# Attention with a mixture of experts: the products with V in two groups of steps per piece instead of four or five

## The chip, the cores and the metric

One Trainium2 chip, one of its cores. The metric is the device time of one execution in microseconds (us). TensorE (PE in the profile, PEld for its weight loads), VectorE (DVE), ScalarE (ACT), GpSimd (POOL) and the DMA queues that SyncE issues (SP) run side by side, each through its own instructions in order, and wait for each other by semaphores.

## The reference

```python
scores = scale * np.matmul(q, k.transpose(0, 1, 3, 2))        # q, k, v: (8, 8, 576, 64)
thresh = np.max(scores, axis=-1, keepdims=True) - tau
scores = np.where(scores >= thresh, scores, -1e9)
attn = np.exp(scores - np.max(scores, axis=-1, keepdims=True))
attn = attn / (np.sum(attn, axis=-1, keepdims=True) + 1e-09)
x = np.matmul(attn, v).transpose(0, 2, 1, 3).reshape(8 * 576, 512)
# then, for every row of x: gate = top 2 of 8 experts of
#   x @ w_gate + log1p(exp(x @ w_noise)) * noise, softmax over the two;
# out = sum over the two of weight * (relu(x @ w1[e]) @ w2[e]),  w1[e]: 512x1024, w2[e]: 1024x512
```

## The kernel before

The program has two parts. Attention works on 32 **turns**, one for each batch and pair of heads (4 pairs, 8 batches). A turn has nine **steps**: 576 query rows of two heads are nine tiles of 128 rows, the first of them (the corner) made of the last 64 rows of both heads. The experts' part follows, and its first loads and gathers are mixed into the last turns.

No scheduler reorders anything: every operation is entered in a list under a step number and a phase, and the program is written out step by step, within a step in the order of phases 0, 1, 2, 3, 4, 5, 8, 6, 7. Step g = 9n + s is step s of turn n, and a table entry of 9 or more falls into the next turn: entry 17 is step 8, entry 21 is step 3 of the turn after the next opening. The text below names steps 0 to 8 by that remainder, and lets a turn open with step 8, in which the scores of the next pair's corner stand. In a step stand, with the line that the profile names:

- phase 0: `oev`, a copy of a finished piece of O by ScalarE (L376);
- phase 1: scores of the next tile, four matmuls of 288 columns into one of two buffers `sp` (L256; six for the corner);
- phases 2 to 4: VectorE takes the row maximum (`rowmax`, L267), ScalarE the exponential (L269), VectorE masks the tile of two steps ago (L292), ScalarE makes the threshold (L277);
- phase 5: `avpiece`, `xlpart`, `xev` and the operations of the gate (below);
- phase 8: ScalarE scales q (L173, step 0) and takes the high parts of k and q (L185, `hik` in step 0, `hiq` in step 2), GpSimd the low parts (L186, `lok`, `loq`);
- phase 6: four transposes of the masked tile of three steps ago on TensorE (L304), copied to `pt` by ScalarE (L307; the corner's by L309 and L310 in step 3);
- phase 7: `pcorner` in step 8 (L325, copies L326 and L327) and `prem` in step 2 (L318, copy L319).

**The products with V.** The transposed probabilities of a turn are multiplied with V in two pieces of 320 and 256 columns. A piece is a sum of five products (index `kt`); one of them is a pair of matmuls for the two heads, each on 64 of the 128 columns of the array (L370); the fifth takes 64 rows for each head from `ptr`. `av` gives the steps of the five for each piece, `oev` the steps in which the pieces are copied to `ot`, `xl` the steps in which `ot` is transposed and multiplied with the gate's weights (`xlpart`, L389 and L390), which VectorE scales into rows of x by `rn` (`xev`, L403). GpSimd makes `rn` in step 3 (L344 to L348).

**Four banks.** Everything but the scores goes to four PSUM banks `tp0` to `tp3`. A list of free ones is kept when the program is written: whoever needs a bank takes the one that has been free longest, and a piece of O keeps its bank from its first product to its copy. So the place of `avpiece` and `oev` in the list decides which bank every transposition takes, and for whose copy it waits.

**The gate.** When the four turns of a batch are done, a chain of small operations picks the experts of its rows. Its place hangs on `xl`:

```python
            x = d["xl"][1] + 1
            for i, f in enumerate((gate_sum, gate_abs, gate_exp, gate_soft, gate_max, gate_hot, gate_rank,
                                   gate_slot, gate_slot2)):
                at(G + START["gate"][i] if late else g + x + i + (i > 3), 5, f, b)
            for i in range(2 * NB):
                to = g + x + 11 + i
```

`gate_hot` makes a table `mb` (VectorE `oh` L555, GpSimd `dl` L558 and `mb` L561); `gate_rank` sums it on TensorE (L568, L570). Ten writes to `slot_table` by GpSimd follow, one per step (`gate_put`, L610 and L611). For the last of the eight batches fixed steps are used. The last turn takes its `av`, `oev` and `xl` from another table (`LAST`), which stays as it is.

Of the kernel before, what the change touches and what calls it, by code (L numbers as in the profile page):

```python
# [36 lines left out]
WARM = 10  # L37

SCHED = dict(
    lag=2, mlag=2, lead=1, corner=8, rem=11, norm=11, av=((10, 11, 12, 13, 14), (15, 17, 17, 18, 19)), oev=(15, 20),  # L40
    xl=(16, 22), q=2, k=0, oevp=0, pieces=((0, 320), (320, 576)), order=(0, 1, 2, 3, 4, 5, 8, 6, 7),
    rec=12, xs=4, qsc="act", qs=0)


# [1 line left out]
    av=((11, 11, 12, 12, 12), (12, 12, 12, 12, 12)), oev=(13, 13), xl=(14, 14), rec=13, norm=12)  # L46
# [1139 lines left out]
```

## Time and profile before

| what | value |
|---|---|
| three runs | 1490.91 us median, 1488.62 to 1496.92 |
| the profiled execution | 1492.15 us, of which 1490.4 us lie between the first and the last instruction |
| busy over the span | PE 98%, PEld 80%, DVE 60%, ACT 47%, POOL 59% |
| busy in 300 to 400 us (attention) | PE 98.03, DVE 83.50, ACT 84.41, POOL 57.72 us of 100 |
| busy in 880 to 960 us (experts) | PE 80.00, DVE 34.23, ACT 16.95, POOL 44.50 us of 80 |
| mean granted clock of TensorE | 0.994 |

A matmul in 32-bit floats shows as two records, so one product with V (two matmuls) shows as four. Matmuls overlap: the duration in a row is longer than the distance to the next row, and the distance from start to start is what an operation costs. The first experts' matmul (L871) starts at 603.67 us; everything that the change moves lies before it.

### The profile page before, as it was taken

How to read it: one execution, taken by the hardware profiler on the slowest of the kernel's cores; microseconds unless marked ns; L12 is line 12 of the kernel's file. 1: busy time of each engine (PE TensorE's matmuls, PEld its weight loads, DVE VectorE, ACT ScalarE, POOL GpSimd, SP SyncE). 2: the span in 40 equal slices, each digit the busy share in tenths (PEclk: the TensorE clock that was granted, in tenths of full speed). 3: DMA queues.
4: the chain of work that ended last, by engine and by line, in shares of the span. 5: the costliest groups of instructions: out<-in, count | busy, mean ns of one | idle time of the engine just before them, and what ended most of it. 6: DMA issues, size and time to landing. Idle time of an engine off the chain costs nothing. (4 is left out here: it accounts for less than half of the span.)

```text
span 1490.4 us, 25728 instructions
## 1 busy us (share of the span) xinstructions
PE 1453.8 (98%) x8750; PEld 1195.9 (80%) x8750; DVE 896.4 (60%) x2477; ACT 706.5 (47%) x1447; POOL 882.8 (59%) x1205
## 2 busy tenths in 40 slices
PE   9999999999999997998999999999999999999995
PEld 6776676766666675787998988989989989989884
DVE  8888888887888889653554354444444543453320
ACT  7887888887888887422222132222222221231210
POOL 3346565656565678877376576576575574665612
PEclk9999999999999999999999999999999999999998
DMA  7768686867686664335155155254353352452422
GB/s 200 186 193 193 168 211 171 209 186 194 175 205 172 159 164 114 76 87 106 43 101 119 36 114 112 53 115 92 66 108 84 85 111 54 92 121 43 71 29 32
DMA packets 137748, 180.67 MB, mean 121 GB/s; under 512 B 61304, under 2 KB 70480, under 8 KB 136592
## 3 DMA queue, kind: packets, MB, share of 16 engines
q1 hardware_dynamic: 106816, 139.05, 35.1%
q0 software_dynamic: 30800, 39.95, 16.6%
q8 instruction: 71, 1.16, 0.4%
q14 instruction: 61, 0.50, 0.1%
HBM read 83.33 MB, written 40.74 MB: 83 GB/s over the span
## 5 line engine op out<-in xcount | busy, mean ns | idle before, releaser
L269 ACT ACTIVATE e<-ns,nm 128x576 f32<-128x576 f32 x288 | 223.2, 775 | 44.1 <-DVE ns L267 41.3
L292 DVE SCALAR_TENSOR_TENSOR p<-ns,thr,e 128x576 f32<-128x576 f32 x256 | 224.0, 875 | 21.5 <-ACT thr L277 20.8
L267 DVE TENSOR_SCALAR_CACHE_REDUCE ns<-sp 128x576 f32<-128x576 f32 x288 | 214.2, 744 | 20.5 <-PE sp L256 18.2
L304 PEld LDWEIGHTS tp<-ident,p 128*128 128x128 f32 x1024 | 110.2, 143 | 100.8 <-ACT ot L376 22.6
L307 ACT ACTIVATE pt<-tp 128x512 f32<-128x512 f32 x256 | 151.0, 590 | 54.1 <-PE tp L304 53.2
L370 PE MATMUL tp<-pt,vt 128*64 128x256 f32 (+1 forms) x1024 | 175.9, 427 | 0.0
L304 PE MATMUL tp<-ident,p 128*128 128x128 f32 x1024 | 167.6, 286 | 1.3 <-DVE p L292 1.3
L256 PE MATMUL sp<-ks,qh 128*128 128x288 f32 x496 | 159.8, 336 | 4.4 <-DVE ns L267 4.3
L913 POOL DMA_INDIRECT out<-m_y,ix x54 | 89.8, 1664 | 100.5 <-DVE m_y L951 86.5
L256 PE MATMUL sp<-ks,ql 128*128 128x288 f32 x496 | 138.4, 295 | 0.0
L186 POOL TENSOR_TENSOR lok<-kr,hik 128x640 fp32r<-128x640 f32 x31 | 57.1, 1841 | 136.8 <-ACT hik L185 124.1
L913 POOL DMA_INDIRECT out<-m_y,sx x43 | 69.8, 1623 | 106.7 <-DVE m_y L894 82.8
L841 POOL DMA_INDIRECT m_vt<-x_rows,ix x102 | 102.5, 1005 | 41.2 <-issue 27.5
L841 POOL DMA_INDIRECT m_zeros<-x_rows,ix x102 | 101.7, 997 | 36.4 <-issue 30.3
L841 POOL DMA_INDIRECT m_xg<-x_rows,ix x100 | 99.5, 995 | 29.9 <-issue 27.2
L873 ACT ACTIVATE m_p<-m_tp 128x384 fp32r<-128x384 f32 (+1 forms) x66 | 33.2, 503 | 143.2 <-PE m_tp L871 143.2
L256 PEld LDWEIGHTS sp<-ks,qh 128*128 128x128 f32 x496 | 93.8, 189 | 6.9 <-DVE ns L267 6.2
L611 POOL DMA_INDIRECT slot_table<-pay,sl x80 | 86.3, 1079 | 17.8 <-issue 11.1
L256 PEld LDWEIGHTS sp<-ks,ql 128*128 128x128 f32 x496 | 94.4, 190 | 0.0
L894 DVE TENSOR_SCALAR m_y<-m_sp,gw 128x512 f32<-128x512 f32 (+1 forms) x43 | 32.2, 750 | 101.8 <-PE m_sp L892 97.2
L370 PEld LDWEIGHTS tp<-pt,vt 128*64 128x64 f32 x1024 | 56.8, 135 | 42.8 <-issue 25.4
L874 DVE SCALAR_TENSOR_TENSOR m_p<-m_tp,m_p 128x384 fp32r<-128x384 f32 (+1 forms) x66 | 37.8, 574 | 59.7 <-ACT m_p L873 59.5
(385 smaller groups left out, 3607.9 us busy)
## 6 DMA issues: line engine op xcount, KB each, us to landing
m_qr<-w SPq DMA_DIRECT2D x85, 256.0 KB
qh<-hiq SPq DMA_DIRECT2D x124, 144.0 KB
ql<-loq SPq DMA_DIRECT2D x124, 144.0 KB
m_kr<-w SPq DMA_DIRECT2D x43, 256.0 KB
kr<-k SPq DMA_DIRECT2D x32, 320.0 KB
out<-zeros SPq DMA_DIRECT2D x19, 512.0 KB
qr<-q SPq DMA_DIRECT2D x32, 288.0 KB
vt<-v SPq DMA_DIRECT2D x8, 1152.0 KB
```

What stands on the lines that cost most here:

```text
L186: nc.gpsimd.tensor_tensor(lo, x, hi.bitcast(F32), op=ALU.subtract)
L256: nc.tensor.matmul(o, q_, k_, start=(i == 0), stop=(i == len(parts) - 1))
L267: nc.vector.tensor_scalar(ns, sp[:, :, 0:HALF], -1.0 / math.sqrt(D), None, op0=ALU.mult, op1=ALU.min, accum_out=nm)
L269: nc.scalar.activation(e, ns, AF.Exp, bias=nm, scale=-1.0)
L292: nc.vector.scalar_tensor_tensor(p, ns, thr, e, op0=ALU.is_le, op1=ALU.mult, accum_out=ssum[n][:, c:c + 1])
L304: nc.tensor.transpose(tp[:, kt, :], p[:, 128 * kt:128 * kt + 128], ident)
L307: nc.scalar.activation(pt[n][:, s, :, c0:c0 + 128], tp, AF.Copy)
L370: nc.tensor.matmul(o[64 * s:64 * s + 64, 0:c1 - c0], w, x, start=(kt == 0), stop=(kt == 4))
L611: st = nc.gpsimd.indirect_dma_start(out=table, out_offset=bass.IndirectOffsetOnAxis(ap=d["sl"][0:m, i, c:c + 1], axis=0), in_=d["pay"][0:m ...
L841: self.nc.gpsimd.indirect_dma_start(out=xg[:, j, :], out_offset=None, in_=x4, in_offset=bass.IndirectOffsetOnAxis(ap=ix[:, kk:kk + 1], axi ...
L874: nc.vector.scalar_tensor_tensor(hl[:, 0:n], ps[:, 0:n], 0.0, hh[:, 0:n].bitcast(F32), op0=ALU.max, op1=ALU.subtract)
L913: st = self.nc.gpsimd.indirect_dma_start(out=out, out_offset=bass.IndirectOffsetOnAxis(ap=idx, axis=0), in_=y, in_offset=None, compute_op= ...
```

## The change

The ten products of a turn move into four groups, the copies of O and the second part of x come one or two steps earlier.

```diff
 SCHED = dict(
-    lag=2, mlag=2, lead=1, corner=8, rem=11, norm=11, av=((10, 11, 12, 13, 14), (15, 17, 17, 18, 19)), oev=(15, 20),
-    xl=(16, 22), q=2, k=0, oevp=0, pieces=((0, 320), (320, 576)), order=(0, 1, 2, 3, 4, 5, 8, 6, 7),
+    lag=2, mlag=2, lead=1, corner=8, rem=11, norm=11, av=((11, 11, 13, 13, 13), (15, 15, 17, 17, 17)), oev=(14, 18),
+    xl=(16, 21), q=2, k=0, oevp=0, pieces=((0, 320), (320, 576)), order=(0, 1, 2, 3, 4, 5, 8, 6, 7),
     rec=12, xs=4, qsc="act", qs=0)
```

By steps of a turn: products stood in steps 1 to 6, 8, and 0 (two in steps 1 and 8, one in each of the others); now two stand in step 2, three in step 4, two in step 6 and three in step 8. The copy of the second piece moves from step 2 to step 0, that of the first from step 6 to step 5, the second part of x from step 4 to step 3. With `xl`, the gate's chain and the writes of x and of `slot_table` come one step earlier for the first seven batches.

**TensorE, the sum of the gate.** Before, in the turn in which the first batch is ranked: the end of step 1's products, step 2 with its transposes, the scores of step 3, and then the sum of `mb`.

```order
L370 MATMUL tp3_1736<-pt1_1512,vt1_614 64x320 x2
L304 MATMUL tp1_1786<-ident_85,p5_1688 128x128 x4
L318 MATMUL tp0_1792<-ident_85,p2_1501 128x128
...
L256 MATMUL sp0_1798<-ks0_1407,qh0_110 128x288
L256 MATMUL sp0_1798<-ks0_1407,ql0_112 128x288
L568 LDWEIGHTS tri_133
L568 MATMUL tp2_1811<-mb0_136,tri_133 128x48
```

And now: step 1's transposes (it has no product), the scores of step 2, the sum, and only then step 2's products and transposes.

```order
L304 MATMUL tp3_1745<-ident_85,p5_1694 128x128 x4
L256 MATMUL sp1_1751<-ks0_1410,qh0_110 128x288
L256 MATMUL sp1_1751<-ks0_1410,ql0_112 128x288
...
L568 LDWEIGHTS tri_133
L568 MATMUL tp2_1764<-mb0_136,tri_133 128x48
...
L370 MATMUL tp1_1779<-pt1_1519,vt1_619 64x320 x4
L304 MATMUL tp0_1800<-ident_85,p5_1694 128x128 x4
```

The sum has moved ahead of step 2's products, transposes and `prem`.

**GpSimd, what the sum reads.** Before, around `mb` of the same batch:

```order
L538 TENSOR_TENSOR nl0_1655<-gc0_1644,lgs0_1566 128x40
L186 TENSOR_TENSOR lok0_1697<-kr1_1397,hik0_1696 128x640
L558 TENSOR_TENSOR dl0_1764<-mx0_1722 128x5
L561 TENSOR_TENSOR mb0_136<-oh0_1762 128x40
L337 TENSOR_SCALAR ssum1_1455<-ssum1_1455 128x9
L186 TENSOR_TENSOR loq0_1771<-qr1_1398,hiq0_1770 128x576
```

And now:

```order
L538 TENSOR_TENSOR nl0_1632<-gc0_1621,lgs0_1543 128x40
L186 TENSOR_TENSOR lok0_1712<-kr1_1402,hik0_1711 128x640
L558 TENSOR_TENSOR dl0_1742<-mx0_1697 128x5
L561 TENSOR_TENSOR mb0_136<-oh0_1740 128x40
L580 TENSOR_SCALAR gs0_1776<-e20_1771 128x5
L337 TENSOR_SCALAR ssum1_1452<-ssum1_1452 128x9
L186 TENSOR_TENSOR loq0_1785<-qr1_1403,hiq0_1784 128x576
```

`mb` stays behind `lok`, which stands in step 0 and reads ScalarE's `hik`.

**ScalarE, which copy frees which bank.** Before, in a turn without the gate, from the copy of step 1's transposes to the corner's in step 3:

```order
L307 ACTIVATE pt0_4104<-tp2_4314 128x4x128
L376 ACTIVATE ot1_4176<-tp1_4190 128x256
L269 ACTIVATE e1_4328<-ns1_4326,nm0_4301 128x576
L277 ACTIVATE thr0_4302<-nm0_4301,atau_105 128x2
L185 ACTIVATE hiq0_4339<-qr0_3953 128x576
L307 ACTIVATE pt0_4104<-tp3_4355 128x4x128
L319 ACTIVATE ptr0_4105<-tp2_4361 128x512
L269 ACTIVATE e2_4376<-ns2_4372,nm1_4373 128x576
L309 ACTIVATE pt1_4391<-tp1_4393 128x4x64
```

And now:

```order
L307 ACTIVATE pt0_4121<-tp1_4314 128x4x128
L269 ACTIVATE e1_4327<-ns1_4325,nm0_4306 128x576
L277 ACTIVATE thr0_4307<-nm0_4306,atau_105 128x2
L185 ACTIVATE hiq0_4341<-qr0_3959 128x576
L307 ACTIVATE pt0_4121<-tp2_4357 128x4x128
L319 ACTIVATE ptr0_4122<-tp0_4363 128x512
L269 ACTIVATE e2_4378<-ns2_4374,nm1_4375 128x576
L309 ACTIVATE pt1_4400<-tp2_4402 128x4x64
```

Before, the corner's transposes of step 3 took bank `tp1`, which the copy of O had freed earlier; now they take `tp2`, the bank of step 2's own transposes, which ScalarE's last copy but one before them frees. The copy of O has left this stretch for step 0.

## The prediction

> **What bounds the kernel now.** I read the busy times by stretch first (the table above): in attention TensorE is busy 98 of 100 us, the others 58 to 84. Then the waits of TensorE between 100 and 600 us. A row gives who waited for whom, the sum, how often, and the longest:
>
> ```profile
> PE sp L256 <- DVE ns L267: 5.2, 9, 2.3
> PE tp L325 <- DVE xr L403: 3.1, 3, 1.6
> PE tp L568 <- POOL mb L561: 1.3, 1, 1.3
> ```
>
> These few us in 500 say that TensorE sets the pace and hardly waits. So I read its timeline over one turn (start, duration, what); the time from start to start is what counts:
>
> ```profile
> 313.23 0.38 PE L256 MATMUL sp<-hik,qd 128*128 128x288 f32 x1
> 315.74 0.38 PE L256 MATMUL sp<-ks,qh 128*128 128x288 f32 x1
> ...
> 319.81 0.38 PE L256 MATMUL sp<-ks,qh 128*128 128x288 f32 x1
> 320.29 0.30 PE L256 MATMUL sp<-ks,ql 128*128 128x288 f32 x1
> 320.52 0.76 PE L370 MATMUL tp<-pt,vt 128*64 128x320 f32 x4
> 321.21 0.65 PE L304 MATMUL tp<-ident,p 128*128 128x128 f32 x4
> 322.05 0.38 PE L256 MATMUL sp<-ks,qh 128*128 128x288 f32 x1
> 323.45 0.66 PE L304 MATMUL tp<-ident,pr 128*128 128x128 f32 x4
> 323.87 0.38 PE L256 MATMUL sp<-ks,qh 128*128 128x288 f32 x1
> 324.34 0.29 PE L256 MATMUL sp<-ks,ql 128*128 128x288 f32 x1
> 324.47 0.27 PE L389 MATMUL tp<-ident,ot 128*128 128x128 f32 x1
> 326.43 0.38 PE L256 MATMUL sp<-ks,qh 128*128 128x288 f32 x1
> 328.23 0.38 PE L256 MATMUL sp<-ks,qh 128*128 128x288 f32 x1
> 329.92 0.38 PE L256 MATMUL sp<-ks,qh 128*128 128x288 f32 x1
> 331.46 0.38 PE L256 MATMUL sp<-hik,qd 128*128 128x288 f32 x1
> ```
>
> The turn opens at 313.23 and the next at 331.46: 18.23 us, of which step 8 takes 2.51, step 2 2.24, step 5 1.80, step 6 1.69, step 7 1.54. A step of attention's first turn, which has no product yet, and the products of the last turn, which stand in a row already, price the rest:
>
> ```profile
> 20.81 0.38 PE L256 MATMUL sp<-ks,qh 128*128 128x288 f32 x1
> 21.81 0.40 PE L256 MATMUL sp<-ks,qh 128*128 128x288 f32 x1
> ...
> 609.18 1.30 PE L370 MATMUL tp<-pt,vt 128*64 128x320 f32 x8
> 610.41 0.66 PE L304 MATMUL tp<-ident,p 128*128 128x128 f32 x4
> 612.66 0.76 PE L370 MATMUL tp<-ptr,vt 64*64 64x320 f32 x4
> 613.35 1.95 PE L370 MATMUL tp<-pt,vt 128*64 128x256 f32 x16
> ```
>
> A step without a product takes 1.00. One product of 320 columns takes 0.69 (320.52 to 321.21), two in a row 1.23 (609.18 to 610.41): the second costs 0.54, one from `ptr` behind them 0.69. By the columns, 0.43 and about 0.58 with 256.
>
> **Part 1: fewer groups on TensorE.** The matmuls are the same; what goes is the entry into the 64-column form and the way out. After a score's last matmul a product starts 0.23 later (320.29 to 320.52), the 128-column transposes of O 0.13 (324.34 to 324.47). The steps become, in us: 8: 2.51 + 0.58 = 3.09; 0 and 1: 1.00 each; 2: 2.24 + 0.54 = 2.78; 3: 1.00 and three blocks of x, 2.0 (step 7 has two blocks for 0.54; the third, narrower one I estimate at 0.4 to 0.5 with its change of form); 4: 1.80 + 0.54 + 0.69 = 3.03; 5: 1.00; 6: 1.69 + 0.43 = 2.12; 7: 1.54. Sum 17.56, that is 0.67 less than 18.23. Over 30 turns this would be -20 us, if nothing else waited.
>
> A rule of the Trainium skill bears on this: TensorEngine Tiling (Array Packing), Key Properties, says that changing the tiling mode drains TensorE, so grouping should pay. The 0.23 against 0.13 agrees. By this rule alone the time would be that of the first rival below.
>
> **Part 2: ScalarE's copies and the bank of step 3.** ScalarE works without a pause from step 8's copy to step 2's. First and last of 15 rows, and two between:
>
> ```profile
> 315.91 0.60 ACT L307 ACTIVATE pt<-tp 128x512 f32<-128x512 f32 x1 [0.57 <-PE tp L304]
> ...
> 318.39 0.72 ACT L185 ACTIVATE hik<-kr 128x640 fp32r<-128x640 f32 x1
> ...
> 320.64 0.38 ACT L376 ACTIVATE ot<-tp 128x256 f32<-128x256 f32 x1
> 320.90 0.78 ACT L269 ACTIVATE e<-ns,nm 128x576 f32<-128x576 f32 x1
> ...
> 322.33 0.59 ACT L307 ACTIVATE pt<-tp 128x512 f32<-128x512 f32 x1
> ```
>
> From 315.91 to 322.92 it needs 7.01. The change keeps the same 15 operations (the copy of O only moves forward among them, 0.26 from its start to the next), and the first waits for step 8's transposes, which come 0.58 later behind the third product: 2.68 + 0.58 = 3.26 after the opening. So step 2's copy ends at 10.27. TensorE would reach the corner's transposes of step 3 at 3.09 + 1.00 + 1.00 + 2.78 + 2.0 - 0.42 = 9.45 (0.42 is 323.45 to 323.87). Before, they took a bank that the copy of O had freed; now they need the bank that this copy empties, and wait 0.82. The turn is then 10.27 + 0.42 + 3.03 + 1.00 + 2.12 + 1.54 = 18.38: the 0.67 is gone, and 0.15 more. Behind the waiting L304 stand all matmuls of steps 3 and 4, so nothing hides it. In quiet turns (16 of 30) this makes +2 us; an error of 0.1 us in the sum gives 0 to +4.
>
> **Part 3: the gate's sum comes too early.** In six turns of the middle, TensorE sums `mb`. Before:
>
> ```profile
> 107.47 0.38 PE L256 MATMUL sp<-hik,qd 128*128 128x288 f32 x1
> ...
> 116.91 0.20 PE L568 MATMUL tp<-mb,tri 128*128 128x48 bf16 x1
> ...
> 117.14 0.49 PE L370 MATMUL tp<-pt,vt 128*64 128x320 f32 x2
> ...
> 113.42 1.56 POOL L186 TENSOR_TENSOR lok<-kr,hik 128x640 fp32r<-128x640 f32 x1 [0.93 <-ACT hik L185]
> 114.93 0.72 POOL L558 TENSOR_TENSOR dl<-mx 128x5 f32<-128x5 f32 x1
> 116.04 0.27 POOL L561 TENSOR_TENSOR mb<-oh 128x40 bf16<-128x40 f32 x1 [0.39 <-DVE oh L555]
> ```
>
> `mb` is done 8.84 after the opening (116.31), and TensorE comes to it at 9.44, in step 3: 0.6 to spare. Now the sum stands in step 2, which TensorE reaches at 3.09 + 1.00 + 1.00, and its place behind the scores 0.60 later: 5.69. But `mb` on GpSimd stays behind `lok`, and `lok` behind ScalarE's `hik`, which ends at 5.16 + 0.72 before and 0.58 + 0.26 later now (step 8's copy is later, the copy of O stands ahead): 6.72. Then `lok` 1.56, `dl` 0.72 and `mb` 0.27 with the gaps of these rows (1.51 from `lok` to `dl`): done at 9.4. VectorE's `oh` comes a step earlier too and is no longer last. TensorE waits 3.7 us. From there: 0.23 to the products (116.91 to 117.14), 1.23 for two, 0.84 for the transposes and `prem` (321.21 to 322.05): step 3 starts at 11.70, the turn ends 2.0 + 3.03 + 1.00 + 2.12 + 1.54 later, at 21.4, against 18.23 and the sum's 0.15, 18.4. So +3.0 in each of six turns, +18; with `dl` at `mb`'s 0.27 or `lok` at 2.0 it is +15 to +21.
>
> Such a wait also costs clock. After the waits of the turn that opens at 144.09, none of them longer than 1.6 (the second row above), the granted clock (0.50 in this row) was halved for one stretch:
>
> ```profile
> 150.10:153.40 3.30, 3.30 (x14) 2.14 (x16) 3.30 (x9) 3.26 (x9) 2.80 (x6) 0.50 0.01 1
> ...
> 300.00:400.00 100.00, 98.03 (x721) 68.51 (x722) 83.50 (x239) 84.41 (x179) 57.72 (x108) 1.00 0.69 179
> ```
>
> That costs up to 1.65 us. In the second row, with a wait of the same length at 371 us, the clock stayed full, so I take half of the six: +5, bounds 0 and +10. The Trainium skill (TensorE: Matmul & The Clock Gate, Part 1) states half clock after an idle window of about 3.4 us; by it all six would pay, +10. The row shows that less idle time can do.
>
> **Part 4: what else moves.** (a) The ten writes to `slot_table` come a step earlier on GpSimd, ahead of one more of its own operations, and still stand before `rn` in step 3. VectorE waits there:
>
> ```profile
> DVE xr L403 <- POOL spacer L610: 16.1, 6, 4.0
> ```
>
> Six turns, 16.1 us; the wait stays, and the 0.53 that ScalarE had in hand before step 3's transposes (322.92 to 323.45) goes: 6 x 0.53 = +3, bounds -2 (the writes start earlier and are done earlier) and +6. (b) For the seventh batch TensorE already waits 1.3 for `mb`, with GpSimd full of gathers; a step earlier it waits longer: +2, bounds 0 and +5. (c) The writes of x on SP's queue and VectorE's rows of x come earlier; VectorE is busy 84 of 100 and has the long step 4 to catch up. Its `xev` waits for TensorE as before: 0. The last turn keeps its own table.
>
> **Sum.** 2 + 18 + 5 + 3 + 2 = +30 us. The profiled execution took 1492.15 us (1490.4 within the span), 1.2 above the median of the runs: 1522 by its own time, and **1521** beside the median 1490.91. By its own bounds the case runs from +11 to +47, 1502 to 1538.
>
> **Rivals.**
> 1. Faster: TensorE alone sets the pace. It needs ScalarE's copy of step 2 ready by 9.45 and `mb` by 5.69. For it: TensorE waits for almost nothing now. Against: 15 rows of ScalarE that leave no gap, and an `mb` that ends 8.84 after the opening even now. 30 turns x -0.67 = -20: 1471. It decides where the copy comes 0.67 sooner than I have it and the sum doesn't wait.
> 2. The bank binds, the sum doesn't wait (if `lok` were ready sooner): 2 + 6 x 0.15 + 3 + 2 = +8: 1499.
> 3. The sum waits, the bank doesn't (if ScalarE's row is shorter when the copy of O moves): 22 turns x -0.67 = -15, and 18 + 5 + 2: +10, 1501. With the clock never halved 1496.
> 4. The half clock in every turn of the gate, and longer waits for `rn`: +47, 1538 or more.
>
> **Chances.** My case 0.65, rival 1 0.08, 2 0.10, 3 0.10, 4 0.07. What a measurement of this kernel tells from no change is about 0.5%, 7.5 us: from 1483 to 1498 is the same. Rival 1 is faster: 0.08. Rivals 2 and 3 lie on the line, half on each side: same 0.10 and, with my case's lowest corner, 0.12. Slower 0.80. The range 1496 to 1538 leaves out rival 1, the upper half of 4 and a tail of my case.
>
> **What would show it.** Right: L304 on `pr` (step 3) waits some 0.8 for ACT `pt` in quiet turns of 18.4; `PE L568 <- POOL mb` becomes the longest wait of TensorE, seven times 3 us or more; step 4 near 3.0, step 0 near 1.0. Wrong: quiet turns of 17.6, or an L568 without a wait. I would be wrong by a size if the clock falls more than once after a wait, or if step 3 takes another bank than the one read from the order.

## The result, and the profile after

| | before | after |
|---|---|---|
| median of four runs, us | 1491.32 (1488.62 to 1496.92) | 1530.74 (1528.09 to 1532.58) |
| the profiled execution, its span, us | 1492.15, 1490.4 | 1528.09, 1526.3 |
| mean granted clock of TensorE | 0.994 | 0.983 |

The ratio of the times is 1.0269, with a 95% interval of 1.0249 to 1.0288: slower by 39 us, where 1521 was forecast. Measured from opening to opening (the rows `sp<-hik,qd`), the turns show where the 35.9 us between the two spans lie. A gate turn is one with the gate's sum, the turn ahead is the one before it, and a put turn is the second one behind it: there VectorE's rows wait for `rn`, which stands on GpSimd among the ten writes.

| stretch | before, us | after, us | difference |
|---|---|---|---|
| 9 quiet turns, 18.23 and 18.39 to 18.41 each | 164.1 | 165.6 | +1.5 |
| 6 turns ahead of a gate turn | 109.4 | 115.1 | +5.7 |
| 6 gate turns, 18.38 and 22.64 to 24.18 each | 110.3 | 140.8 | +30.5 |
| 6 put turns | 117.6 | 113.6 | -4.0 |
| the start, the first and the last turns, up to L871 | 102.3 | 102.4 | +0.1 |
| the experts' part | 886.7 | 888.9 | +2.2 |

The busy times by stretch, of the changed kernel between 300 and 400 us (each engine's busy us in the order PE, PEld, DVE, ACT, POOL, then the granted clock): TensorE waits now, and its clock isn't full.

```profile
300.00:400.00 100.00, 93.01 (x673) 68.12 (x673) 75.89 (x223) 76.75 (x164) 57.39 (x112) 0.97 0.64 170
```

The waits of the changed kernel between 100 and 600 us: TensorE's four longest groups, then one of VectorE and one of GpSimd.

```profile
PE tp L304 <- ACT pt L307: 14.6, 19, 0.8
PE tp L568 <- POOL mb L561: 12.6, 5, 2.7
PE sp L256 <- DVE ns L267: 7.7, 14, 0.9
PE tp L568 <- ACT e L573: 5.4, 2, 2.7
...
DVE ab L513 <- POOL lgs L506: 20.9, 7, 3.1
...
POOL rn L347 <- DMA slot_table<-pay,sl: 16.4, 6, 3.3
```

The first row is the forecast wait for ScalarE's copy, the second and the fourth the wait of the gate's sum (where `e` is named, it is the exponential of `dl`, which ends beside `mb`). The third has two halves, and neither was foreseen. In each turn ahead VectorE waits with `ab` (the fifth row), and the row maximum that stands behind it comes late for TensorE's scores. In each gate turn the row maximum stands behind the ten small operations of `gate_max` (L545, L547; from 3.97 to 5.00 us after the opening), and the scores of step 2 wait 0.54. The first turn ahead, which opens at 89.80:

```profile
106.54 0.20 DVE L513 SCALAR_TENSOR_TENSOR ab<-lgs 128x40 f32<-128x40 f32 x1 [3.06 <-POOL lgs L506]
...
107.47 0.40 PE L256 MATMUL sp<-ks,qh 128*128 128x288 f32 x1 [0.56 <-DVE ns L267]
```

A quiet turn of the changed kernel, TensorE and then ScalarE (start, duration, what; in brackets the wait and who ended it):

```profile
131.68 0.38 PE L256 MATMUL sp<-hik,qd 128*128 128x288 f32 x1
...
134.76 0.38 PE L256 MATMUL sp<-ks,qh 128*128 128x288 f32 x1
...
142.00 0.66 PE L304 MATMUL tp<-ident,pr 128*128 128x128 f32 x4 [0.81 <-ACT pt L307]
...
150.08 0.38 PE L256 MATMUL sp<-hik,qd 128*128 128x288 f32 x1
...
134.93 0.60 ACT L307 ACTIVATE pt<-tp 128x512 f32<-128x512 f32 x1 [1.15 <-PE tp L304]
...
137.01 0.77 ACT L173 ACTIVATE qr<-qr,scale 128x576 f32<-128x576 f32 x1
...
141.36 0.59 ACT L307 ACTIVATE pt<-tp 128x512 f32<-128x512 f32 x1
```

ScalarE's row goes from 3.25 after the opening to 141.36 + 0.59, that is 10.27, and step 3's transposes of the corner start 0.05 later. The turn has 18.40 us.

A gate turn of the changed kernel: TensorE, GpSimd, and then the busy times and the clock in the 3.41 us up to the sum and in those behind it:

```profile
109.03 0.38 PE L256 MATMUL sp<-hik,qd 128*128 128x288 f32 x1
...
113.08 0.38 PE L256 MATMUL sp<-ks,qh 128*128 128x288 f32 x1
...
114.83 0.40 PE L256 MATMUL sp<-ks,qh 128*128 128x288 f32 x1 [0.54 <-DVE ns L267]
...
118.31 0.20 PE L568 MATMUL tp<-mb,tri 128*128 128x48 bf16 x1 [2.69 <-POOL mb L561]
...
115.83 1.54 POOL L186 TENSOR_TENSOR lok<-kr,hik 128x640 fp32r<-128x640 f32 x1 [3.37 <-ACT hik L185]
117.33 0.71 POOL L558 TENSOR_TENSOR dl<-mx 128x5 f32<-128x5 f32 x1
118.00 0.26 POOL L561 TENSOR_TENSOR mb<-oh 128x40 bf16<-128x40 f32 x1
...
114.64:118.05 3.41, 0.80 (x4) 0.66 (x5) 3.31 (x10) 3.41 (x7) 2.22 (x3) 1.00 0.43 118
118.05:121.47 3.42, 3.16 (x17) 1.58 (x17) 2.55 (x7) 0.87 (x3) 3.05 (x6) 0.50 0.91 207
```

`mb` is done at 118.26, 9.23 after the opening; TensorE's step 1 took 1.75 instead of 0.97 (113.08 to 114.83, waiting for VectorE); it stood ready for the sum at 115.62, waited 2.69, and then worked for 3.42 us at half clock.

### The profile page after: what moved, and what is told of

Its sections match the earlier page's. It is cut to its first block, busy times and chain, and to the rows that moved or that the text cites. A ratio compares the mean times of both kernels' runs of the same rounds, so it can differ in the third digit from the quotient of the medians.

```text
span 1526.3 us, 25726 instructions
## 1 busy us (share of the span) xinstructions
PE 1452.4 (95%) x8750; PEld 1218.9 (80%) x8750; DVE 883.6 (58%) x2477; ACT 703.0 (46%) x1447; POOL 876.9 (57%) x1205
## 5 line engine op out<-in xcount | busy, mean ns | idle before, releaser
L292 DVE SCALAR_TENSOR_TENSOR p<-ns,thr,e 128x576 f32<-128x576 f32 x256 | 220.3, 861 | 42.0 <-ACT thr L277 41.2
L304 PEld LDWEIGHTS tp<-ident,p 128*128 128x128 f32 x1024 | 117.5, 145 | 62.8 <-issue 33.8
L370 PE MATMUL tp<-pt,vt 128*64 128x256 f32 (+1 forms) x1024 | 158.5, 432 | 0.0
L186 POOL TENSOR_TENSOR lok<-kr,hik 128x640 fp32r<-128x640 f32 x31 | 50.6, 1633 | 171.3 <-ACT hik L185 160.4
L370 PEld LDWEIGHTS tp<-pt,vt 128*64 128x64 f32 x1024 | 64.0, 139 | 47.2 <-issue 22.9
L611 POOL DMA_INDIRECT slot_table<-pay,sl x80 | 90.2, 1127 | 18.2 <-issue 10.7
L871 PE MATMUL m_tp<-m_pt,m_pt 128*128 128x384 f32 (+1 forms) x396 | 73.6, 343 | 0.0
```

Source lines behind the costliest of these rows:

```text
L186: nc.gpsimd.tensor_tensor(lo, x, hi.bitcast(F32), op=ALU.subtract)
L292: nc.vector.scalar_tensor_tensor(p, ns, thr, e, op0=ALU.is_le, op1=ALU.mult, accum_out=ssum[n][:, c:c + 1])
L304: nc.tensor.transpose(tp[:, kt, :], p[:, 128 * kt:128 * kt + 128], ident)
L370: nc.tensor.matmul(o[64 * s:64 * s + 64, 0:c1 - c0], w, x, start=(kt == 0), stop=(kt == 4))
L611: st = nc.gpsimd.indirect_dma_start(out=table, out_offset=bass.IndirectOffsetOnAxis(ap=d["sl"][0:m, i, c:c + 1], axis=0), in_=d["pay"][0:m ...
L871: nc.tensor.matmul(ps[:, 0:n], w[:, 128 * c:128 * c + 128], x[:, c, 0:n], start=(i == 0), stop=(i == len(ops) - 1))
```

## The experiments

All times are medians; each ratio is to the kernel before, run beside it on the same chip, and is taken over all runs, so that it need not be the quotient of two medians.

| kernel | us | ratio, 95% interval |
|---|---|---|
| 1: after, gate chain in its old place | 1506.31 | 1.0104 (1.0085 to 1.0124) |
| 2: after, only the gate's sum in its old place | 1507.35 | 1.0135 (1.0105 to 1.0165) |
| 3: before, gate chain a step earlier | 1498.21 | 1.0061 (1.0044 to 1.0078) |
| 4: before, only the products moved | 1499.31 | 1.0068 (1.0051 to 1.0084) |
| 5: 1 and the scaling of q moved | 1487.13 | 0.9987 (0.9971 to 1.0004) |
| 6: after, the scaling of q moved | 1509.73 | 1.0125 (1.0093 to 1.0157) |
| 7: before, the scaling of q moved | 1485.57 | 0.9971 (0.9959 to 0.9982) |
| 8: after, `dl` and `mb` on VectorE | 1517.35 | 1.0188 (1.0161 to 1.0215) |
| 9: 5 and two more waits moved | 1473.80 | 0.9886 (0.9858 to 0.9913) |
| 10: 7 and the writes moved | 1483.36 | 0.9955 (0.9939 to 0.9971) |

**1. The gate's chain and the writes back in their old steps.**

```diff
-            x = d["xl"][1] + 1
+            x = d["xl"][1] + 1 + (n < NP - 1)
```

> The changed kernel, but the gate's chain, the writes of x and of slot_table stand one step later, at the steps of the kernel before. Theory (the gate's chain, tied to xl, came a step too early, and the saved form changes are eaten by ScalarE's bank in step 3): TensorE reaches the sum of mb in step 3 about 8.4 us after the opening, mb is done at 9.3, and most of that wait lies within the wait for ScalarE's copy; gate turns about 18.5 instead of 23.5, quiet turns stay at 18.4; about 1492 us, between 1488 and 1498. Rival (the groups themselves cost: long steps starve VectorE and ScalarE): still above 1515.

1506, above the range: three fifths of the loss go, but not all that the theory gave. The gate turns are still 19.4 to 21.0, since the sum waits in its old place too:

```profile
PE tp L568 <- POOL mb L561: 8.5, 7, 1.5
...
PE tp L389 <- ACT pt L307: 1.7, 6, 0.3
```

The new groups leave steps 0 and 1 without a product, so TensorE comes to step 3's sum 8.6 after the opening and not at 9.44, while `mb` is done at 9.7 instead of 8.84. The expectation had such a wait, from 8.4 to 9.3, but put most of it inside the wait for ScalarE's copy. The trace shows one behind the other: with a bank taken by the sum, the transposes of O behind it (L389) wait for that copy, and step 3's transposes of the corner come only after them, at 11.34 instead of 10.32. Three of the six turns also have a stretch at half clock (20.9 to 21.0, the others 19.4). The turns ahead are back at 18.40 and VectorE's `ab` waits 0.8 at most. So of the +5.7 there, the part beyond the quiet turn's growth needs the chain's early place. It needs the new groups as well: in run 3, which has the early place with the old products, these turns keep 18.23, and `ab` waits 0.8.

**2. Only the sum and the two operations behind it back.**

```diff
-                at(... else g + x + i + (i > 3), 5, f, b)
+                at(... else g + x + i + (i > 3) + (i > 5), 5, f, b)
```

> The changed kernel, but only gate_rank, gate_slot and gate_slot2 stand one step later (their old place); the front of the chain and the writes stay early. Theory: the wait of 2.7 us for mb and the halved clock go, the wait of 0.8 us in the turn before each gate turn (scores of step 7 behind VectorE) stays: about 6 us above e1, 1494 to 1503. Rival: as in e1, above 1515.

1507, no faster or slower than the first: missed, and by the same oversight. The L568 row is gone from the waits, but behind the sum the transposes of O wait for ScalarE, up to 1.2 us, so that five gate turns still have 19.4, and the turns ahead keep their 19.2:

```profile
PE tp L389 <- ACT pt L307: 5.9, 7, 1.2
```

**3. The old products, the gate's chain a step earlier.**

```diff
-            x = d["xl"][1] + 1
+            x = d["xl"][1] + (n == NP - 1)
```

> The kernel before with its own products, copies and xl, but the gate's chain, the writes of x and of slot_table one step earlier. Theory: TensorE reaches the sum in step 2 at about 7.2 us after the opening, mb is done at about 8.6: a wait of 1.4 us in six turns, perhaps half clock behind it: 1500 to 1512. Rival (the early chain is harmless, the groups are at fault): within 3 us of the kernel before.

1498, just under the range. Every gate turn grew from 18.38 to 19.73 behind a wait of 1.2 for `mb`, so the early sum costs by itself, without the new groups. It costs less than in the changed kernel because the old products still stood ahead of it, and none of the six waits halved the clock. The put turns became 3.6 us shorter in sum: in this trace the earlier writes are a gain, not a loss.

**4. The products alone in their new steps.**

```diff
-av=((10, 11, 12, 13, 14), (15, 17, 17, 18, 19))
+av=((11, 11, 13, 13, 13), (15, 15, 17, 17, 17))
```

> The kernel before with only the products in the new groups; copies of O, xl and the gate as before. Theory: in quiet turns the wait moves from step 3 to the prem transposes of step 2, whose bank waits for ScalarE's copy of step 1 (about 0.75 us), and a little in step 4; turn about 18.3; 1489 to 1499. Rival (groups at fault): above 1515. Rival 2 (form changes saved and nothing waits): 17.6 per turn, 1472.

1499.3, just over the upper edge. With the copy of O still in step 2 the banks rotate otherwise, and the wait for ScalarE moves to `prem`, 0.5 where 0.75 was expected. The quiet turns have 18.19, those right behind a gate turn 18.47, none near 17.6; the gate turns, of which the expectation says nothing, have 19.16 instead of 18.38:

```profile
PE tp L318 <- ACT pt L307: 10.5, 23, 0.5
```

**5. The first kernel, and ScalarE's row made shorter.** The scaling of q (L173, 0.66 from start to start) leaves step 0 for step 7 of the turn before.

```diff
-            at(g + d["qs"], 8, scale_q, n + 1)
+            at(g - 2 if n > 1 else g, 8, scale_q, n + 1)
```

> The changed kernel with the gate chain and its writes one step later (the kernel of the first experiment), and ScalarE's scaling of the next pair's q moved from step 8 to step 7 of the turn before, so out of ScalarE's row between the copy of step 8 and the copy of step 2. Theory (that row of 7.01 us sets the quiet turn): the row is 0.66 shorter, the wait of the corner's transposes in step 3 falls from 0.8 to 0.2 or less, quiet turns go from 18.39 to about 17.7, and over some 28 turns the time falls by 15 to 20 from 1506, to 1484 to 1492. Rival (the bank is not what holds step 3, or another copy takes its place): quiet turns stay at 18.2 to 18.4, time 1500 to 1507.

1487, in the range, and every quiet turn has 17.73 or 17.74 where it had 18.40: 0.66, the length of the operation that was taken out. The wait in step 3 falls from 0.8 to 0.2, as forecast. That ScalarE's row set the turn is shown.

**6. The changed kernel with that move alone.**

> The changed kernel with nothing but the scaling of q moved from step 8 to step 7 of the turn before. Theory: quiet turns near 17.7 instead of 18.39; in the turns of the gate hik, lok and mb come 0.66 earlier as well, so the wait for mb falls from 2.7 to about 2.0 and may halve the clock less often. 1502 to 1514 instead of 1531. Rival (ScalarE's row is not the reason): 1526 to 1532.

1509.7, in the range. Quiet turns 17.73, the sum's wait 2.0 instead of 2.7. Beyond its purpose this run prices the clock, since the same wait fell with and without a half clock. The openings and the sum of the first and second gate turn, and the busy times in stretches of 3.41 us (PE first, the clock is the third value from the end):

```profile
106.21 0.38 PE L256 MATMUL sp<-hik,qd 128*128 128x288 f32 x1
...
114.79 0.18 PE L568 MATMUL tp<-mb,tri 128*128 128x48 bf16 x1 [1.98 <-POOL mb L561]
...
182.75 0.38 PE L256 MATMUL sp<-hik,qd 128*128 128x288 f32 x1
...
191.31 0.18 PE L568 MATMUL tp<-mb,tri 128*128 128x48 bf16 x1 [1.97 <-POOL mb L561]
...
110.29:113.70 3.41, 1.97 (x14) 1.60 (x13) 3.41 (x20) 3.39 (x8) 1.36 (x1) 1.00 0.52 202
113.70:117.11 3.41, 2.32 (x23) 1.56 (x22) 3.34 (x11) 2.02 (x6) 1.46 (x6) 1.00 0.83 187
188.79:192.20 3.41, 1.44 (x16) 1.03 (x17) 3.38 (x7) 2.17 (x5) 2.15 (x3) 1.00 0.45 108
192.20:195.61 3.41, 3.41 (x17) 2.47 (x14) 1.93 (x9) 2.11 (x6) 2.56 (x5) 0.51 0.95 226
```

The stretches are cut where the clock changes: in each of these traces its changes lie on one grid of 3.413 us. The first wait falls across a line of the grid (1.44 and 1.09 us without work on the two sides) and the clock stays full; that turn has 20.55 us. The second lies within one window (1.97 without work), the next window runs at half clock, and the turn has 22.14. So one window at half clock costs 1.59 us, and the fifth gate turn, with two, cost 2.81 (23.36).

**7. The kernel before with that move.**

> The kernel before with the same move of the scaling of q alone. Theory: there TensorE has its own 18.23 us of work in a turn and ScalarE's copy of step 2 is ready 0.53 before it is wanted, so a shorter row changes nothing: quiet turns 18.23, time 1487 to 1493. Rival (a shorter row of ScalarE is a gain by itself, in any kernel): 1476 to 1484.

1485.6, a little under the range. The quiet turns keep 18.23 to the hundredth, so the theory holds where it was meant; but the put turns lose 6.9 us in sum (117.6 to 110.7), which the expectation had left out: the low parts of k and q come some 0.7 earlier on GpSimd, and the waits of `rn` there fall from 19.8 to 13.2.

**8. The gate's `dl` and `mb` on VectorE.**

```diff
-        eng.tensor_tensor(dl, ...)
+        vec.tensor_tensor(dl, ...)
...
-        eng.tensor_tensor(mb[b % 2][:, 0:NB, :], ...)
+        vec.tensor_tensor(mb[b % 2][:, 0:NB, :], ...)
```

> The changed kernel with the gate's dl and mb on VectorE right behind oh, instead of on GpSimd behind lok. Theory (the gate's sum waits because mb stands behind hik and lok): mb is done near 7.1 after the opening instead of 9.24, the wait of L568 falls from 2.7 to about 1.3, the turns of the gate from 22.6 to 24.2 down to 19.5 to 21, with fewer stretches at half clock: 1508 to 1518 instead of 1531. Rival (it waits for something else, the bank or the gate's own operations on VectorE, and only the name of the last one changes): 1526 to 1533.

1517, in the range, with a wait of 1.9 instead of 1.3; the gate turns have 20.4 to 23.3, mostly above the 19.5 to 21 expected. `mb` no longer stands behind `lok` in a queue, and yet waits it out. The first gate turn, and then the turn of the seventh batch, where `lok` had ended before:

```profile
115.82 0.16 DVE L558 TENSOR_TENSOR dl<-mx 128x5 f32<-128x5 f32 x1
115.94 1.52 DVE L561 TENSOR_TENSOR mb<-oh 128x40 bf16<-128x40 f32 x1
...
115.87 1.54 POOL L186 TENSOR_TENSOR lok<-kr,hik 128x640 fp32r<-128x640 f32 x1 [3.39 <-ACT hik L185]
...
589.74 0.20 DVE L561 TENSOR_TENSOR mb<-oh 128x40 bf16<-128x40 f32 x1
...
588.07 1.54 POOL L186 TENSOR_TENSOR lok<-kr,hik 128x640 fp32r<-128x640 f32 x1 [0.22 <-ACT hik L185]
```

Forty columns took 1.51 to 1.54 us on VectorE in all six gate turns, until `lok` ended on GpSimd, and 0.20 where `lok` did not run beside it (0.26 on GpSimd itself). The Trainium skill (SBUF — State Buffer, section "SBUF: two separate sides") says that an operation of VectorE with two inputs from SBUF and one of GpSimd that reads SBUF exclude each other for a whole instruction; the rows agree.

**9. The fifth kernel without the waits that it still showed.** The sum stands one step later, where TensorE doesn't reach it before `mb`, and no write to `slot_table` stands right ahead of `rn` on GpSimd. What `rn` waited for can be read from the traces of the two kernels and of runs 1 to 8: in six turns of each, the fourth copy of `rn` carries a wait for the landing of the write that was issued last ahead of it, and it starts 3.1 to 7.5 us after that write's issue.

```diff
-                at(... else g + x + i + (i > 3), 5, f, b)
+                at(... else g + x + i + (i > 3) + (i > 5), 5, f, b)
...
-                to = g + x + 11 + i
+                to = g + x + 11 + i + (i > 4)
```

> The kernel of the fifth experiment (products in the new groups, gate chain in its old place, scaling of q moved) with two waits taken away that its trace still shows: the gate's sum and the two steps behind it stand one step later (0.8 of waiting in each of six turns), and the sixth to tenth write to slot_table one step later, so that none stands on GpSimd right ahead of rn (4.0 of waiting on GpSimd, and put turns 9.4 longer in all than six quiet ones). Theory: what grouping the products saves on TensorE, 0.5 to 0.67 a turn, shows once nothing else waits: 1487 - 4 - 7 = about 1476, 1471 to 1482, below the kernel before with the scaling moved (1485.6). Rival (new waits of the same size take their place, as the transposes of O behind the later sum did): 1483 to 1490.

1473.8: the changed groups are now the fastest of all, 15 us under the kernel before beside it. Quiet turns, turns ahead and put turns all have 17.73 to 17.75, gate turns 17.88. First the waits of GpSimd's `rn` for the writes in the fifth kernel; then, in this one, TensorE in step 3 of a quiet turn and `rn` in the same turn, the one behind a gate turn. Its fourth copy (L347) carries no such wait here:

```profile
POOL rn L347 <- DMA slot_table<-pay,sl: 21.0, 6, 4.1
```

```profile
133.41 0.66 PE L304 MATMUL tp<-ident,pr 128*128 128x128 f32 x4 [0.21 <-ACT pt L307]
...
138.80 0.19 POOL L346 COPY rn<-ssum 64x4 f32<-64x4 f32 x1
139.03 0.72 POOL L347 COPY rn<-ssum 64x4 f32<-64x4 f32 x1
```

**10. The control: the old groups with the same moves of q and of the writes.** The sum stays, since it does not wait there.

> The control for the run above: the kernel before with the scaling of q moved, and the sixth to tenth write to slot_table one step later. Theory: its put turns are only 1.3 longer in all than six quiet ones, so this changes nothing that can be measured: 1483 to 1487, quiet turns 18.23. Rival (moving the writes is itself worth what the run above gains): 1474 to 1479.

1483.4, as the theory had it: quiet and put turns 18.23, gate turns 18.38. Beside it the new groups gain 9.6 us by the medians. Between the two spans it is 11.7: 0.50 in each of 28 turns, 14.0 in all; then 3.4 lost in the turn behind them, where the experts' first work is mixed in, 2.9 won from there to the experts' first matmul, and 1.9 lost in the experts' part.

## Why the prediction was right, point by point

The forecast was 1521 and slower; 1530.74 lies 10 above it, inside the range. The two waits that it was built on are there, at nearly the forecast costs. That the sum came no farther off is in part luck: the put turns fell 7 us below their term, against 4.7 us that were in no term and 8 by which the clock's was too small.

- **Part 1, the groups.** Right. Step 2 takes 2.78, step 4 3.03, step 6 2.13, step 8 3.08, steps 0 and 1 0.97 each, against 2.78, 3.03, 2.12, 3.09 and 1.00; step 3 takes 2.13 without its wait, against 2.0. The unstalled turn of 17.56 is seen in run 9: 17.73 with a wait of 0.21. So the first rival's saving exists, and is what runs 9 and 10 differ by; it was not to be had in the change as it was made. The rule of the Trainium skill (TensorEngine Tiling (Array Packing), Key Properties) that a change of the tiling mode drains TensorE agrees with this saving, which by run 9 is 0.71 a turn on TensorE's own row (18.23 less 17.52).
- **Part 2, ScalarE's row.** Right to 0.02 us: the row starts at 3.25 for 3.26, ends at 10.27 for 10.27, the wait is 0.81 for 0.82, the turn 18.40 for 18.38. Run 5 shows the cause.
- **Part 3, the gate's sum.** The mechanism was right: `hik` behind the longer step 8, `lok`, `dl`, `mb`, done at 9.23 for 9.4. TensorE came to the sum at 6.59, not at 5.69, because step 2's scores had themselves waited, behind `gate_max` on VectorE; from 5.69 to the sum's start at 9.28 it is 3.6, for 3.7. So the sign that was named, seven waits of 3 us or more, came as six of 2.7 and one of 1.9. Less the clock at run 6's prices (three turns with one window, three with two: 3 x 1.59 + 3 x 2.81 = 13.2), the six turns cost 17.3 more, against 18.
- **The half clock** is the term that was mis-sized: +5, with bounds of 0 and +10, against 13.2. All six waits halved it, where half of them was taken, and in three turns for two windows. The two turns before with waits alike, one with a drop and one without, were read as an even chance for any wait. On the grid of run 6 they are not alike: the window ahead of the drop at 150.10 held 1.65 us without work, the one around 371 us 1.22. A wait of 2.7 leaves over 1.65 in one window of 3.41 in about four of five places where it can fall (an estimate from these two lengths). The upper bound was too low as well, since it had no second window in it; that the clock falls more than once after a wait was the prediction's own sign of being wrong by a size.
- **A term was missing**: of the +5.7 in the turns ahead, 1.0 is part 2's, and 4.7 were in no step. The second operation of the gate's chain (`ab`, L513) waits on VectorE for GpSimd's `lgs` (L506), one step earlier than before, 3.1 us instead of at most 0.8; behind it in VectorE's queue stands the row maximum, and behind that TensorE's scores, 0.8 us late. The early place and the new groups make this wait together: VectorE comes to `ab` 13.7 after the opening and `lgs` is done at 16.7, against 14.9 and 15.7 in run 3. The prediction moved the chain's sum and its writes step by step, but not the operations ahead of `gate_hot`; of VectorE's earlier work it asked only whether there was room.
- **Part 4 (a)** had the wrong sign: +3 against -4.0, past the lower bound of -2. The bank's wait did not add to the wait for `rn`, which became shorter (19.8 us in six turns before, 16.4 after): the fourth copy started 3.4 to 5.0 after the issue of the write that it waits for, where it had been 5.0 to 7.5. Why that write landed sooner is not shown. Run 3 has the same without the new products, -3.6; but run 6, with the early writes, has put turns 2.7 longer in sum than run 5, with the late ones, so the sign holds for these traces and no further.
- **Part 4 (b) and (c).** From the first turn and the last turns to the experts' first matmul the sum is +0.1; the +2 for the seventh batch is not seen as such, though its sum waits 1.9 instead of 1.3. The experts' part differs by +2.2, with 884.8 to 889.0 in the runs above in no order; that rest stays open.

By the terms: forecast 2 + 18 + 5 + 3 + 2 = 30; measured 1.5 + 5.7 in the quiet turns and the turns ahead, 17.3 + 13.2 in the gate turns, -4.0 in the put turns, 2.3 elsewhere: 35.9 before rounding. Added up, the terms' own bounds give +13 to +46, not the +11 to +47 that the prediction states.

## What to carry to other kernels

Regrouping work on the busiest engine pays only as far as the next engine's row allows: before moving it, add up that row between the two points where the engines meet, and move one operation out of it together with the change. Of a chain that is moved a step, follow every link to the queue that it waits for and to what stands behind the waiting one; the link that was overlooked here held up VectorE, and cost 4.7 us. Then take the new waits away one by one from the trace: the same regrouping went from 2.7% slower to 1.1% faster by four shifts of a step or two.

## What the runs showed of the hardware that was not expected

- **The clock's grid.** In the twelve traces, with idle time taken as the gaps between the matmul records, the granted clock changed on a grid of 3.413 us. From 18 to 590 us all 22 windows with more than 1.64 us of idle time were followed by a window at half clock, none of 1921 with less than 1.19 was, and of 26 between these four were. The line is not sharp: later in the traces ten windows with 1.66 to 1.83 us kept the full clock behind them, and from 18 to 1400 us none of the 40 with more than 1.84 us did. The Trainium skill (TensorE: Matmul & The Clock Gate, Part 1) has the free-running window of 3413 ns, and the traces agree; its idle window of about 3.4 us as the condition they do not bear out: about half a window of idle time, in one window of the grid, is enough.
- **The second window.** Where the window at half clock held another pause of 0.41 us or more, the next ran at half clock too (all five cases up to 590 us, in the changed kernel and in runs 6 and 8); with 0.26 or less it was back to full. One later window, in run 9, held 0.58 and the next was full, so this line is not sharp either.
- **VectorE beside GpSimd.** Forty columns took 1.52 us on VectorE while GpSimd worked on 640 columns, and 0.20 when it did not (run 8): moving this small operation to another engine did not free it from the one that it left.
- **An indirect write's landing.** The fourth small copy of `rn` waited 0.7 to 5.2 us for the landing of the indirect write issued last ahead of it, and started 3.1 to 7.5 us after that write's issue (60 cases in ten traces). The wait stands in the program, on that copy and not on the first three; why it was put there is open.
